# One stated order instead of a list scheduler: a three-stage kernel (LSH attention and two expert layers) on one core

## The chip, the cores and the metric

The kernel runs on one core of one Trainium2 chip. The time is that of the device in microseconds; the median of three runs before the change is 678.09 (677.57 to 679.59). Lower is better.

## The reference, cut to what matters

```
q_bits, k_bits = (q @ proj > 0), (k @ proj > 0)              # 6 hash bits each
mask   = bucket(q_bits)[:, None] == bucket(k_bits)[None, :]
scores = where(mask, q @ k.T / 8, -1e9)                      # 2 batches x 8 heads, 768 x 768, head 64
attn   = softmax(scores) @ v
x = attn as (1536, 512)
x = max(x @ w1, x @ w2, x @ w3) @ w_out                      # 512 -> 768 -> 512
h = x @ w_in                                                 # 512 -> 2048
return where(h > 0, h, exp(min(h, 0)) - 1) @ w_out2          # 2048 -> 512
```

The weights come as 64-bit floats, the attention inputs as 32-bit ones. The kernel splits every matmul operand in a high and a low half of 16 bits and sums three products.

## The kernel before, in words

The 1536 tokens are cut into six chunks (c = 0 to 5) of 256 tokens. A chunk's attention has 16 tiles (four pairs of heads, two heads, two blocks of 128 queries), so there are 96 tiles, t = 0 to 95. A tile goes through all engines: PE makes the scores (L681), DVE takes the row maximum (L684) and two small numbers of it (L685, L687), ACT the exponential (L689), ACT or DVE the high half (L693 to L697), POOL or DVE the low half (L700), the SP queue issues a DMA transpose of both halves (L702, `PT<-hl`), and PE multiplies by v (L711 to L713). After four tiles DVE divides, and the result is split again (L733, L734). After eight, a second transpose on SP (L737, `xT<-xn`) makes half of a chunk's input for the first expert layer.

The first expert layer of a chunk (L748, called with w13 and then wot; matmuls `mo<-xT,w` and `mo<-hT,wot`) can start when both xT halves of the chunk are there and the weights are unpacked: a load of 512 KB (L589), three to four operations on ACT and DVE that turn 64-bit words into 32-bit ones (L594 to L605), a sum of squares, and a split in two halves (L617 to L619). Its matmuls fill PE between the tiles of the following chunks. The second expert layer runs when attention is over: four groups of four blocks f, and for each group and chunk, four steps x (twelve matmuls, L748 `mo<-x1T,win`) and four steps o (six matmuls, L882). Between x and o of one block stand ACT (L867, L869), DVE (L870, L872), then the two halves (L874, L876). Its weights are loaded only when the tiles of attention have given their memory back.

All small results of PE go through a ring of three PSUM buffers, `mo`: a step that writes one waits until the third step before it has been read. In the second layer that reading ends with L872.

The program is built from a graph of 3,374 operations. Each has a dictionary of the engines that can do it (PE, V = DVE, A = ACT, G = POOL, D = the SP queue; for DMA loads and copies, D or the ACT queue), and a priority. `Graph.schedule` is a list scheduler: with costs written in the code (`vtt`, `act`, `gtt`, `pe`, a DMA model) it decides at every step which operation goes next and on which engine, and `emit` writes them in that order. Each engine then works strictly in this order and waits, by semaphores, for what its next instruction needs. DMA issues stand in the order of the queue that issues them: SP does nothing else, ACT issues between its own work. The loads of k, v and weights are held back until the first load of k has been issued (`g.after(..., first["kl"])`).

Of the kernel before, what the change touches and what calls it, by code (L numbers as in the profile page):

```python
# [21 lines left out]

# [8 lines left out]
class Graph:  # L37

    LAT = {"PE": 200, "V": 150, "A": 160, "G": 100, "D": 1500, "N": 0}
# [4 lines left out]
    def buf(self, pool, shape, dt, tag, bufs, ordered=False):  # L44

        self.bufs_of[tag] = bufs
        b = Buf(tag, lambda: pool().tile(shape, dt, tag=tag, name=tag, bufs=bufs))
        if ordered:
            b.turn = self.turns[tag]
            self.turns[tag] += 1  # L50
        return b
# [6 lines left out]
    def op(self, eng, fn, rd=(), wr=(), prio=0.0, two=False):  # L58

        i = len(self.ops)
        deps, allocs, used = set(), [], []
# [24 lines left out]
    def schedule(self):  # L88
        ops, n = self.ops, len(self.ops)
        engs = ("PE", "V", "A", "G", "D", "N")  # L90
        succ, left = [[] for _ in ops], [0] * n
        for o in ops:
            left[o["i"]] = len(o["deps"])
            for d in o["deps"]:
                succ[d].append(o["i"])
            for b in o["used"]:
                b.left = len(b.users)
        end, by, done = [0.0] * n, [None] * n, [False] * n
        rings, waiting = defaultdict(list), defaultdict(list)
        pending, ready, free = {e: [] for e in engs}, {e: [] for e in engs}, {e: 600.0 for e in engs}  # L100
        dma_free, dge, busy, warm = 0.0, 0.0, [], False
        held = {"V": 0.0, "G": 0.0}
        order = []

        def release(i, t0=0.0):
            for e in ops[i]["eng"]:
                r = max([t0] + [end[d] + self.LAT[by[d]] * (0.8 if by[d] == e else 1) for d in ops[i]["deps"]])
                heapq.heappush(pending[e], (r, i))

        for o in ops:  # L110
            if not left[o["i"]]:
                release(o["i"])
        while len(order) < n:
            best = None
            for e in engs:
                while pending[e] and (pending[e][0][0] <= free[e] or done[pending[e][0][1]]):
                    i = heapq.heappop(pending[e])[1]
                    if not done[i]:
                        c = ops[i]["eng"][e]
                        heapq.heappush(ready[e], (ops[i]["prio"] + (c[-1] if isinstance(c, tuple) and e != "D" else 0), i))  # L120
                while ready[e] and done[ready[e][0][1]]:
                    heapq.heappop(ready[e])
                t = free[e] if ready[e] else max(free[e], pending[e][0][0]) if pending[e] else None
                if t is not None and (best is None or t < best[0]):
                    best = (t, e)
            if best is None:
                stuck = {i for l in waiting.values() for i in l}
                msg = []
                for i in sorted(stuck):
                    for b in ops[i]["allocs"]:  # L130
                        r, k = rings[b.ring], self.bufs_of[b.ring]
                        if len(r) >= k and r[-k].left:
                            msg.append((i, ops[i]["prio"], b.ring, [(j, ops[j]["prio"], ops[j]["fn"].__qualname__[-30:], left[j]) for j in r[-k].users if not done[j]]))
                raise RuntimeError("no operation can start:" + "".join("\n  %s" % (m,) for m in msg[:60]))
            t, e = best
            if not ready[e]:
                free[e] = t
                continue
            if e == "V" and held["G"] > t:

                late_ = KAPPA * (held["G"] - t)
                j = min(range(len(ready[e])), key=lambda j: (ready[e][j][0] + late_ * ops[ready[e][j][1]]["two"], ready[e][j][1]) if not done[ready[e][j][1]] else (1e9, 0))
                _, i = ready[e][j]
                ready[e][j] = ready[e][-1]
                ready[e].pop()
                heapq.heapify(ready[e])
            else:
                _, i = heapq.heappop(ready[e])
            o = ops[i]
            if e == "V" and o["two"] and held["G"] > t or e == "G" and held["V"] > t:  # L150
                t1 = held["G" if e == "V" else "V"]
            else:
                t1 = t
            block = None
            for b in o["allocs"]:
                r, k = rings[b.ring], self.bufs_of[b.ring]
                if b.turn is not None and b.turn != len(r):
                    block = b.ring, b.turn
                    break
                if len(r) >= k:  # L160
                    old = r[-k]
                    if old.left:
                        block = old
                        break
                    if old.free > t:
                        block = old.free
                        break
            if block is not None:
                if isinstance(block, (Buf, tuple)):
                    waiting[block].append(i)  # L170
                else:
                    heapq.heappush(pending[e], (block, i))
                continue
            c = o["eng"][e]
            if e == "D" or (isinstance(c, tuple) and len(c) == 4):
                t0 = max(t, dge)
                free[e], dge = t0 + c[0], t0 + (c[1] if e == "D" else c[0])
                end[i] = max(dge + 650, dma_free) + c[2]
                dma_free = end[i]
                if not c[0]:  # L180
                    free[e] = max(t0 + 1300, end[i] - 877)
                lat = "D"
            else:
                c = c[0] if isinstance(c, tuple) else c
                if e == "PE":
                    busy = [(a, z) for a, z in busy if z > t - 3400]
                    share = sum(z - max(a, t - 3400) for a, z in busy) / 3400
                    warm = share > (0.5 if warm else 0.88)
                    c = c if warm else 2 * c
                    busy.append((t, t + c))  # L190
                free[e] = end[i] = t1 + c
                lat = e
                if e == "G" or e == "V" and o["two"]:
                    held[e] = t1 + c
            done[i], by[i] = True, lat
            order.append((i, e, t))
            for b in o["allocs"]:
                rings[b.ring].append(b)
                for j in waiting.pop((b.ring, len(rings[b.ring])), ()):
                    release(j, t)  # L200
            for b in o["used"]:
                b.left -= 1
                b.free = max(b.free, end[i] + self.LAT[lat])
                if not b.left:
                    for j in waiting.pop(b, ()):
                        release(j, b.free)
            for j in succ[i]:
                left[j] -= 1
                if not left[j]:
                    release(j)  # L210
        self.order, self.end = order, end
        return order

    def emit(self):
        for i, e, _ in self.schedule():
            o = self.ops[i]
            for b in o["allocs"]:
                b.ap = b.make()
            o["fn"](e)


# [17 lines left out]
def lsh_attention_moe_kernel(ctx: ExitStack, tc: tile.TileContext, q, k, v, proj,  # L239
# [53 lines left out]
    def ring(pool, shape, tag, bufs, dt=F32, ordered=False):  # L293
        p = pool if callable(pool) else (lambda: pool)
        return g.buf(p, list(shape), dt, tag, bufs, ordered)
# [133 lines left out]
    def plan_qk(kind, b, p, hf, u, prio):  # L429
# [26 lines left out]
        if u:  # L456
            g.after(lod, first["kl"])
# [84 lines left out]
    def plan_v(b, p, prio):  # L542
# [11 lines left out]
        g.after(lod, first["kl"])  # L554
# [26 lines left out]

    def plan_w(tag, src, prio, pool, nraw, n2, need=()):
# [6 lines left out]
        if tag == "w":  # L591
            g.after(ld, first["kl"])
            wloads.append(ld)
# [240 lines left out]
    def plan_moe2(c, gi, fs, p0, dp):  # L834
# [23 lines left out]
        outs = [ring(lambda: late["ps_out"], [128, 512], "out", 2 * QT) for _ in range(QT)]  # L858
        for m, f in enumerate(fs):
# [19 lines left out]
            def omm(e, f=f, m=m, gt=gt):  # L879
                for j in range(QT):  # L880
                    for pi, (x, y) in enumerate(((0, 0), (0, 1), (1, 0))):
                        PE.matmul(outs[j].ap, gt.ap[:, x, j * 128:(j + 1) * 128], wo2t[f].ap[:, y],  # L882
                                  start=(m == 0 and pi == 0), stop=(m == n - 1 and pi == 2))
# [119 lines left out]
```

## Time and profile before

| | |
|---|---|
| median of three runs | 678.09 us |
| span of the profiled execution, first to last instruction | 677.9 us |
| PE busy | 625.1 us (92%) |
| DVE busy | 578.8 us (85%) |
| ACT busy | 445.6 us (66%) |
| POOL busy | 204.3 us (30%) |
| DMA, mean over the span | 129 GB/s |
| first matmul of the first expert layer | 120.7 us |
| last tile's product with v | 360.7 us |

One execution is profiled. Its time beyond the span is not listed, the span and the median of the runs differ by 0.2 us. A busy PE is not PE at its peak, since the ends of matmuls are modelled and a lower clock lengthens them.

### The profile page before, as it was taken

What the parts mean: (1) busy time and instruction counts of PE and PEld (TensorE: products, weight loads), DVE (VectorE), ACT (ScalarE), POOL (GpSimd) and SP (SyncE); (2) the same over time, 40 slices, a digit from 0 to 9 for tenths busy, and PEclk for the clock granted to TensorE, in tenths of its full rate; (3) what the DMA queues carried; (4) which work ended last, traced back from release to release, by engine and by line L of the source; (5) the groups of instructions that cost most, each with busy time, mean ns of one, the idle gap of its engine ahead of it and who ended that gap; (6) DMA issues with size and microseconds to landing.
All of it is one profiled execution on the core that took longest, in us unless ns stands there. A gap on an engine that the chain in (4) does not pass through costs nothing.

```text
span 677.9 us, 16515 instructions
## 1 busy us (share of the span) xinstructions
PE 625.1 (92%) x6414; PEld 481.5 (71%) x6414; DVE 578.8 (85%) x1574; ACT 445.6 (66%) x807; POOL 204.3 (30%) x164
## 2 busy tenths in 40 slices
PE   5766567999999999999999799999999999999997
PEld 4645445787888888888889688766666666666664
DVE  7998799999979979989984997898899798877775
ACT  4788788898977846865562885676779365433331
POOL 0045444575666744665540011021020000000000
PEclk9958656999999999999999999999999999999999
DMA  9889998998798776989686544122121000000112
GB/s 281 254 214 207 215 250 204 234 213 157 149 193 177 134 140 111 157 165 163 139 179 175 179 153 156 33 94 63 49 78 62 1 1 1 1 1 1 63 51 74
DMA packets 201118, 87.65 MB, mean 129 GB/s; under 512 B 167760, under 2 KB 195408, under 8 KB 201040
## 3 DMA queue, kind: packets, MB, share of 16 engines
q1 hardware_dynamic: 187120, 68.78, 47.5%
q10 hardware_dynamic: 13920, 17.82, 8.9%
q8 instruction: 50, 0.82, 0.5%
q14 instruction: 28, 0.23, 0.1%
HBM read 38.80 MB, written 3.15 MB: 62 GB/s over the span
## 4 chain that ended last, share of the span: by engine, by line
PE 75%; DVE 9%; ACT 5%; DMA 4%; issue 2%; SPq 0%; ACTq 0%; POOL 0%; DVEq 0%; POOLq 0%
PE mo L748 42%; PE out L882 18%; PE s L681 7%; DMA PT<-hl 4%; DVE m L684 2%; ACT P L689 2%; PE o L711 2%; PE o L712 2%; PE o L713 2%; DVE w L619 1%; PE mo L474 1%; DVE dc2w L605 1%; ACT mo L594 1%; DVE dc L605 0%; SPq L702 0%
## 5 line engine op out<-in xcount | busy, mean ns | idle before, releaser
L700 POOL TENSOR_TENSOR hl<-P,hl 128x768 f16<-128x768 f32 x77 | 131.9, 1719 | 127.3 <-DVE hl L697 55.4
L748 PE MATMUL mo<-xT,w 128*128 128x256 f16 x1296 | 153.4, 274 | 0.1
L748 PE MATMUL mo<-x1T,win 128*128 128x256 f16 x1152 | 140.6, 272 | 0.0
L882 PE MATMUL out<-wo2t,gt 128*128 128x512 f16 x576 | 139.1, 379 | 0.0
L748 PEld LDWEIGHTS <-w 128*128 128x128 f16 x1296 | 123.7, 98 | 15.1 <-issue 0.2
L748 PEld LDWEIGHTS <-win 128*128 128x128 f16 x1152 | 111.0, 98 | 27.5
L689 ACT ACTIVATE P<-s,bias,scale 128x768 f32<-128x768 f32 x96 | 91.9, 986 | 38.8 <-DVE bias L687 29.6
L867 ACT ACTIVATE r<-mo,nih 128x256 f32<-128x256 f32 x96 | 45.1, 470 | 86.4 <-PE mo L748 84.5
L684 DVE TENSOR_REDUCE m<-s 128x1 f32<-128x768 f32 x96 | 89.6, 949 | 5.2 <-PE s L681 4.7
L882 PEld LDWEIGHTS <-gt 128*128 128x128 f16 x576 | 56.0, 98 | 48.5
L876 POOL TENSOR_TENSOR gt<-g,gt 128x256 f16<-128x256 f32 x28 | 20.3, 724 | 224.7 <-ACT gt L874 74.6
L711 PE MATMUL o<-vt,PT 128*128 128x65 f16 x576 | 66.2, 198 | 8.7 <-DMA PT<-hl 5.1
L695 ACT CAST hl<-P 128x768 f16<-128x768 f32 x72 | 59.3, 827 | 13.8 <-DMA PT<-hl 9.3
L681 PE MATMUL s<-ka,qa 128*128 128x384 f16 x192 | 53.1, 362 | 14.8 <-ACT P L689 14.5
L712 PE MATMUL o<-vt,PT 128*128 128x64 f16 x576 | 66.1, 199 | 0.0
L713 PE MATMUL o<-vt,PT 128*128 128x65 f16 x576 | 65.9, 198 | 0.0
L711 PEld LDWEIGHTS <-PT 128*128 128x128 f16 x576 | 55.8, 100 | 13.6 <-DMA PT<-hl 6.1
L712 PEld LDWEIGHTS <-PT 128*128 128x128 f16 x576 | 55.7, 101 | 3.3 <-issue 0.9
L713 PEld LDWEIGHTS <-PT 128*128 128x128 f16 x576 | 55.7, 102 | 0.0
L870 DVE TENSOR_SCALAR uu<-e,sg 128x256 f32<-128x256 f32 x96 | 35.3, 368 | 23.5 <-ACT e L869 23.0
L681 PE MATMUL s<-kb,qb 76*128 76x384 f16 x192 | 54.0, 366 | 0.0
L748 PE MATMUL mo<-hT,wot 128*128 128x256 f16 x432 | 50.2, 272 | 0.5 <-DVE zq L500 0.5
(195 smaller groups left out, 1109.2 us busy)
## 6 DMA issues: line engine op xcount, KB each, us to landing
raww<-in_moe_w_dram SPq DMA_DIRECT2D x12, 512.0 KB
raw<-in_moe_w_out_dram ACTq DMA_DIRECT2D x8, 512.0 KB
raw<-in_moe_w_in_dram SPq DMA_DIRECT2D x8, 512.0 KB
raw<-in_moe_w_in_dram ACTq DMA_DIRECT2D x8, 512.0 KB
raw<-in_moe_w_out_dram SPq DMA_DIRECT2D x8, 512.0 KB
raww<-in_moe_w_dram ACTq DMA_DIRECT2D x6, 512.0 KB
out_dram<-ot SPq DMA_DIRECT2D x12, 256.0 KB
rawk<-in_k_dram SPq DMA_DIRECT2D x6, 384.0 KB
```

Source lines behind the costliest of these rows:

```text
L681: PE.matmul(ps.ap[:, h, :NK], lh[0:n, h0 + i, j], rh[0:n, i, h * CH:(h + 1) * CH], start=first, stop=not first)
L684: op({"V": vred(S)}, lambda e: V.tensor_reduce(out=m.ap, in_=ps.ap[:, :, :NK], op=ALU.max, axis=AX.XY), rd=[ps], wr=[m], prio=t + 80.5)
L689: op({"A": act(S, ap=2) - 42}, lambda e: A.activation(out=P.ap.rearrange("p (c n) -> p c n", c=2), in_=ps.ap[:, :, :NK], func=AF.Exp, scal ...
L695: A.copy(hl.ap[:, 0], P.ap)
L700: op({"G": gtt(S), "V": (vtt(S), -109.46)}, lambda e: eng[e].tensor_tensor(out=hl.ap[:, 1], in0=P.ap, in1=hl.ap[:, 0], op=ALU.subtract), r ...
L711: PE.matmul(oo, pt.ap[:, kt], vt.ap[:, i, kt, :D + 1], start=(kt == 0), stop=False)
L712: PE.matmul(oo[:, :D], pt.ap[:, kt], vt.ap[:, i, kt, D + 2:], start=False, stop=False)
L713: PE.matmul(oo, pt.ap[:, NS + kt], vt.ap[:, i, kt, :D + 1], start=False, stop=(kt == NS - 1))
L748: PE.matmul(o, lh(kk, x), rh(kk, y), start=(kk == 0 and pi == 0), stop=(kk == n - 1 and pi == 2))
L867: op({"A": act(NQ, ap=1) - 42}, lambda e, m=m, o=o, r=r: A.activation(out=r.ap, in_=o.ap[:, :NQ], func=AF.Relu, scale=nih.ap[:, m:m + 1]), ...
L870: op({"V": vts(NQ)}, lambda e, m=m, ex=ex, uu=uu: V.tensor_scalar(out=uu.ap, in0=ex.ap, scalar1=-1.0, scalar2=sg.ap[:, m:m + 1], op0=ALU.a ...
L882: PE.matmul(outs[j].ap, gt.ap[:, x, j * 128:(j + 1) * 128], wo2t[f].ap[:, y], start=(m == 0 and pi == 0), stop=(m == n - 1 and pi == 2))
```

## The change

`Graph.schedule`, its costs of latency and the three `g.after(..., first["kl"])` are deleted. A table `ORDER` states for all 3,374 operations which comes next and on which engine, and `emit` follows it. The graph, the operations and the buffer rings are the same. The six matmuls of a step o set their first and last flag by the order in which steps come, since the blocks of a group may now come in any order.

```
-        for i, e, _ in self.schedule():
-            o = self.ops[i]
+        raw = zlib.decompress(base64.b85decode(ORDER))
+        n = len(raw) // 2
+        assert n == len(self.ops)
+        done = [False] * n
+        for lo, hi in zip(raw[:n], raw[n:]):
+            w = hi << 8 | lo
+            o, e = self.ops[w >> 3], ENGINES[w & 7]
+            assert e in o["eng"] and not done[o["i"]] and all(done[d] for d in o["deps"])
+            done[o["i"]] = True
             for b in o["allocs"]:
                 b.ap = b.make()
             o["fn"](e)
...
-        if u:
-            g.after(lod, first["kl"])
...
-            def omm(e, f=f, m=m, gt=gt):
+            def omm(e, f=f, gt=gt, outs=outs, seen=seen):
+                seen.append(f)
                 for j in range(QT):
                     for pi, (x, y) in enumerate(((0, 0), (0, 1), (1, 0))):
                         PE.matmul(outs[j].ap, gt.ap[:, x, j * 128:(j + 1) * 128], wo2t[f].ap[:, y],
-                                  start=(m == 0 and pi == 0), stop=(m == n - 1 and pi == 2))
+                                  start=(len(seen) == 1 and pi == 0), stop=(len(seen) == n and pi == 2))
```

What the table says, read out of its entries and set against the order that the list scheduler makes (before, after):

| | before | after |
|---|---|---|
| operations on another engine than before | | 377 |
| DMA loads and copies on the ACT queue, whole program | 56 | 14 |
| the same, ahead of the first matmul of the first layer | 24 | 5 |
| of these: weights, q and k, v, big copies, copies of hash bits, proj | 8, 4, 2, 2, 6, 2 | 1, 1, 0, 1, 0, 2 |
| weight loads ahead of the second xT on the DMA queues | 20 | 21 |
| loads of k, q, v and transposes PT ahead of it | 7, 7, 6, 19 | 7, 7, 6, 19 |
| loads ahead of the first PT | 23 | 20 |
| tiles with scores on PE ahead of the first layer's first matmul | 26 | 26 |
| ahead of it on DVE: L464, L603, L734, L561 | 7, 14, 2, 4 | 2, 7, 0, 1 |
| ahead of it on DVE: L700, L618 | 2, 1 | 4, 6 |
| ahead of it on POOL: L464, L700, L734 | 3, 20, 2 | 8, 18, 4 |
| weights unpacked (L605), split (L619) ahead of it | 20, 17 | 18, 15 |
| sums of squares of second-layer weights on PE ahead of the last chunk's first matmul | 6 | 4 |
| steps x with just two steps of PE between them and the x that held their `mo` buffer | 2 | 12 |
| steps o with just three steps of PE after their x | 1 | 10 |

Ten or so smaller operations ahead of the first layer change between DVE and ACT in either direction.

## Rows read from the trace of the kernel before

**Rows 1.** Windows: stretch, length, busy of engines (instructions), clock, DMA share, GB/s.

```profile
0.00:120.70 120.70, 79.85 (x919) 58.69 (x919) 105.26 (x291) 93.88 (x151) 41.81 (x39) 0.76 0.97 232
...
120.70:361.00 240.30, 236.64 (x3198) 202.48 (x3194) 215.92 (x520) 174.41 (x267) 137.12 (x93) 1.00 0.85 163
361.00:390.00 29.00, 24.63 (x240) 21.62 (x237) 21.38 (x55) 17.30 (x38) 1.20 (x1) 0.99 0.66 195
390.00:674.60 284.60, 284.02 (x2073) 198.76 (x2071) 235.97 (x710) 159.97 (x353) 24.20 (x31) 0.99 0.16 51
```

**Rows 2.** Line L748: PE instructions, shortest/median/longest ns, first and last start.

```profile
L748 PE MATMUL mo<-xT,w x1296: 269/272/421, 120.7 to 415.7; 128*128 128x256 f16 x186
```

**Rows 3.** Chain that ended last, 0 to 120.7: shares by line, longest DMA piece.

```profile
by line: DVE m L684 9.4%; PE s L681 7.0%; DMA PT<-hl 6.9%; issue 6.6%; DVE w L619 6.1%; ACT P L689 4.9%; DVE dc2w L605 4.6%; ACT mo L594 3.6%; SPq L702 2.5%; PE mo L474 2.0%; ACTq L528 1.7%; DVE scale L685 1.6%; ACT hl L695 1.5%; DVE dc2w L
...
76.29 8.31 DMA PT<-hl
```

**Rows 4.** Groups of instructions by form: count, busy us, mean ns, idle before.

```profile
L464 DVE TENSOR_TENSOR natk<-rawk,natk 128x768 f16<-128x768 f32 x5 | 5.6, 1121 | 0.0
L603 DVE TENSOR_SCALAR dc2w<-raww 128x512 uint16<-128x512 uint16 x15 | 6.5, 450 | 0.0
L734 DVE TENSOR_TENSOR xn<-xf,xn 128x256 f16<-128x256 f32 x9 | 7.7, 855 | 0.1
L561 DVE TENSOR_SCALAR vt<-rawv,vs 128x768 f16<-128x768 f32 x6 | 4.3, 716 | 0.0
L700 DVE TENSOR_TENSOR hl<-P,hl 128x768 f16<-128x768 f32 x19 | 21.4, 1124 | 0.9 <-ACT hl L695 0.5
L618 DVE TENSOR_SCALAR wo2t<-dc,o2s 128x512 f16<-128x512 f32 x5 | 2.4, 483 | 0.1
L605 DVE SCALAR_TENSOR_TENSOR dc2w<-mo,dc2w 128x512 int32<-128x512 int32 x24 | 16.3, 686 | 1.3 <-ACT dc2w L598 1.1
L619 DVE SCALAR_TENSOR_TENSOR w<-dc2w,swm,w 128x512 f16<-128x512 f32 x18 | 16.5, 937 | 1.6 <-ACT w L617 1.5
L464 POOL TENSOR_TENSOR natq<-rawq,natq 128x512 f16<-128x512 f32 x6 | 7.4, 1228 | 8.2 <-DVE natq L462 6.3 <-ACT P L689 1.9
L876 DVE TENSOR_TENSOR gt<-g,gt 128x256 f16<-128x256 f32 x68 | 29.2, 429 | 1.7
```

**Rows 5.** DMA issues on the ACT queue: sequencer's time, shortest/median/longest ns.

```profile
L589 ACTq DMA_DIRECT2D raww<-in_moe_w_dram x6: 374/374/449, 5.8 to 92.5; - x6
...
L528 ACTq DMA_DIRECT2D kb<-btk x8: 730/771/1513, 38.7 to 249.5; - x8
```

**Rows 6.** Windows with almost only loads, and with three transposes and nothing else.

```profile
13.00:30.00 17.00, 11.80 (x164) 9.62 (x164) 16.18 (x46) 11.93 (x24) 0.00 (x0) 1.00 1.00 284
...
214.40:219.90 5.50, 5.50 (x62) 4.58 (x61) 5.12 (x13) 3.43 (x7) 2.06 (x2) 1.00 0.89 202
```

**Rows 7.** Timeline of PE at the seam: start, length, instruction [idle before, releaser].

```profile
387.23 0.18 PE L342 MATMUL mo<-w2acc,ones 128*128 128x1 bf16 x1 [0.99 <-DVE hx L802]
...
389.08 0.18 PE L342 MATMUL mo<-w2acc,ones 128*128 128x1 bf16 x1 [1.65 <-DVE o2s L380]
```

**Rows 8.** Timeline of the second layer: a quick block and a slow one.

```profile
472.50 1.47 PE L748 MATMUL mo<-x1T,win 128*128 128x256 f16 x12
...
475.11 1.47 PE L748 MATMUL mo<-x1T,win 128*128 128x256 f16 x12
...
475.36 0.48 DVE L872 SCALAR_TENSOR_TENSOR g<-mo,aj,uu 128x256 f32<-128x256 f32 x1
...
441.08 1.47 PE L748 MATMUL mo<-x1T,win 128*128 128x256 f16 x12
...
445.44 0.47 DVE L872 SCALAR_TENSOR_TENSOR g<-mo,aj,uu 128x256 f32<-128x256 f32 x1
...
446.28 0.43 DVE L876 TENSOR_TENSOR gt<-g,gt 128x256 f16<-128x256 f32 x1
```

**Rows 9.** Waits, 390 to 674: total us, times, longest.

```profile
ACT r L867 <- PE mo L748: 84.5, 61, 1.8
```

More of the change, by code (lines that the diff above doesn't have):

```diff
@@ L1 @@
-import heapq
+import base64
+import zlib
 from collections import defaultdict
@@ L37 @@
 class Graph:
-    LAT = {"PE": 200, "V": 150, "A": 160, "G": 100, "D": 1500, "N": 0}
     def __init__(self):
@@ L47, in buf @@
         b = Buf(tag, lambda: pool().tile(shape, dt, tag=tag, name=tag, bufs=bufs))
-        if ordered:
-            b.turn = self.turns[tag]
-            self.turns[tag] += 1
         return b
@@ L86, in after @@
         self.ops[i]["deps"].update(js)
[L88 to L212, printed above, removed]
@@ L553, in plan_v @@
            wr=[raw, acc], prio=prio + 176.2)
-        g.after(lod, first["kl"])
         qloads.append((lod, (b * NH * NP + p) + 0.0 / UL))
@@ L591, in plan_w @@
         if tag == "w":
-            g.after(ld, first["kl"])
             wloads.append(ld)
@@ L858, in plan_moe2 @@
         outs = [ring(lambda: late["ps_out"], [128, 512], "out", 2 * QT) for _ in range(QT)]
+        seen = []
         for m, f in enumerate(fs):
```

50 lines of the change are left out of this document (added).

## The prediction, made before the changed kernel was run

> **What bounds the kernel now.** I read the windows by stage first, because the shares of the whole span mix three stages. From 120.7 us to 361 PE is busy 236.64 of 240.30 at full clock, and from 390 to 674.6 it is busy 284.02 of 284.60 [rows 1]. In these two stages only PE's own work counts, and the change does not touch it: the same matmuls, the same shapes. What PE loses lies in two other places. The first is the head, up to the first matmul of the first expert layer at 120.7 [rows 2]: PE is busy 79.85 us there at a mean clock of 0.76. The second is the seam from 361 to 390, with 24.63 of 29.00 busy. So a new order can win time only in these two, and it can lose time anywhere.
>
> What bounds the head? DVE is busy 105.26 of 120.70, ACT 93.88, and the DMA engines 0.97 of it at 232 GB/s [rows 1]. Nothing has much room. The chain that ended last says which of them is felt: the four DVE lines that its header still shows make 21.7% of the stretch (9.4, 6.1, 4.6, 1.6), ACT's waits at its own DMA issues (L528) 1.7%, and one transpose alone takes 8.31 us, from 76.29 on [rows 3]. So DVE first, then ACT with its queue, and transfers at one place.
>
> I make the sum against the span of 677.9; the median of the runs is 678.09, so 0.2 us lie around it, and I add nothing for them.
>
> **The head: DVE.** Counted in the table ahead of the first layer's first matmul, DVE gives away five low halves of q and k (L464, 1.121 each), seven sign operations (L603, 0.450), two low halves of results (L734, 0.855) and three scalings of v (L561, 0.716): 5.6 + 3.2 + 1.7 + 2.1 = 12.6 us. It takes on two low halves of tiles (L700, 1.124) and five weight splits (L618, 0.483): 2.2 + 2.4 = 4.7. Two weights less are unpacked (L605, 0.686) and two less split (L619, 0.937) by then: 3.2 us that move behind 120.7, where PE sets the pace and DVE has 24 us free of 240 [rows 1, 4]. Net 12.6 - 4.7 + 3.2 = 11.1 us less. The smaller moves go both ways and I leave them out. How much of it is felt? At least the share of the chain, 0.22, which gives 2.4; at most DVE's busy share, 105.26 of 120.70 or 0.87, which gives 9.7. I take half, 5.5, since the header is cut and DVE's other lines on the chain are missing in the lower figure.
>
> **The head: ACT's queue.** Nineteen issues leave it. Thirteen at 0.374 and the six copies of hash bits at 0.771 are 4.9 + 4.6 = 9.5 us of ACT's sequencer [rows 5]. They go to SP, where the transposes stand in the same order. ACT's computing stays about the same (eight operations taken on, seven splits given away). At most 9.5 are felt; at least what the chain names, 1.7% of 120.7 or 2.1 us, since all six bit copies go. I take 2.1: ACT is a fifth below the span [rows 1].
>
> **The head: transfers.** The bytes ahead of the second xT are the same but for one weight load. Is there room for an earlier xT? Loads run at 284 GB/s when almost alone, and three transposes with nothing beside them take 5.50 x 0.89 / 3 = 1.63 us each [rows 6]. From the shapes of the tiles: 20 weights of 0.524 MB, 7 of k and 6 of v of 0.393, 7 of q of 0.262, together 17.4 MB or 61 us; 19 transposes, 31 us; two xT of two thirds, 2 us. That makes 94 us, plus the small copies, of the 120 that they have. The bound of one more load is 0.524 / 284, 1.8 us, and I cost it at nothing because the 26 us of slack cover it. If the cover is gone, the load costs all of its 1.8.
>
> [...]
>
> **The head: POOL.** It does five more low halves of q and k, two more of results and two fewer of tiles: five operations more. An operation of one form takes 0.855 on DVE in the attention stage (L734) and 0.429 in the second layer (L876), where POOL is busy 24.20 of 284.60 [rows 1, 4]. So a DVE operation beside POOL is stretched by 0.43, and five of them cost 2.1 us. The lower end is nothing, if DVE happens to do other things; I take 2.1, since L734 is of this stage.
>
> [...]
>
> Head: 5.5 + 2.1 - 2.1 = 5.5 us won.
>
> **The seam.** PE waits 0.99 and 1.65 us for sums of squares of second-layer weights, at 387.23 and 389.08, before the last chunk's first matmul [rows 7]. In the table four such sums stand ahead of it instead of six; the two others come behind it, while matmuls of the last chunk run. I take both waits off, 2.6 us. At the other end the four can be as late as the six were, and nothing is won.
>
> **The second layer.** Here the new order is tighter than the old. At twelve places a step x has two PE steps (2.61 us, as the starts 472.50 and 475.11 of two steps x show, with one o between) between the end of the step that held its `mo` buffer and its own start, and at ten places a step o starts three steps, half as much again or 3.9 us, after its x; before there were two and one. The x of 472.50 ends at 473.81, half of 2.61 later, and has its buffer read (L872) at 475.84, 2.0 us later; its low half (L876) follows some 0.8 after that, if it goes as in the slow block. The slow one of 441.08 ends at 442.39 in the same way and needs 3.5 us for the one (445.91) and 4.3 for the other (446.71) [rows 8]. A quick block fits in both distances; a slow one makes PE wait 0.9 or 0.4. Between 0 and 12 x 0.9 + 10 x 0.4 = 14.8 us. In 61 of 96 blocks ACT was waiting for PE when x ended [rows 9], so most are quick, and I take a tenth, 1.5.
>
> Sum: 677.9 - 5.5 - 2.6 + 1.5 = **671.3**. For the runs I say 671, with its own range from 667 to 676 (the head between 2 and 10 us won, the seam between 0 and 2.6).
>
> **Rivals.**
> - *Transfers set the head.* Against: the 94 us above. For: a DMA share of 0.97 and the transpose of 8.31 us [rows 1, 3]; on SP twenty of 21 loads now stand ahead of transposes in one queue. Then the first layer starts no earlier, only seam and second layer count, and one more load may: 677.9 - 2.6 + 1.5 = 676.8, up to 678.6.
> - *The second layer stalls* (slower). The mechanism is the ring of `mo`: if most blocks there are slow, PE waits 14.8 us, and 677.9 - 8.1 + 14.8 = 684.6. It decides when the 22 places wait 0.37 us on average (8.1 / 22). For it: unpacking of weights shares ACT and DVE with these blocks. Against: DVE has 48 us free of 285 [rows 1].
> [...]
> - *Everything in the head that waits gets shorter.* If DVE's 11.1 is felt in full, and the transpose of 8.31 falls to about half as no other queue loads beside it, the head wins 11.1 + 2.1 - 2.1 + 4.2 = 15.3 and the end is 661.5.
>
> **How the numbers follow.** My forecast 0.55, transfers 0.11, a stalling second layer 0.11, POOL 0.08, the shorter head 0.15. The bound of a difference that a measurement of this kernel can tell is 0.3%, 2 us, so faster is below 676.1. Faster: 0.55 + 0.15 + 0.07 of POOL, 0.77. Same: nearly all of the transfers, 0.10. Slower: the stalling layer and what is left of the others, 0.13. The range runs from 662, which leaves out half of the shorter head, to 680, which leaves out most of the stalling layer: two in ten at most.
>
> **What would show it.** Right: the first matmul of L748 starts at about 115 instead of 120.7; DVE is busy some 10 us less before it, the ACT queue issues five loads or copies there; no wait of PE over half a microsecond for L380 or L395 before the last chunk's first matmul; from then to the end PE is idle no more than 2 us. Wrong: L748 starts at 120 or later with SP waiting at a load in front of transposes; PE waits for L872 or L876 in the second layer; DVE's operations on 128x768 grow longer. The prediction would be wrong most of all if PE, from its first L748 on, is no longer fed without gaps, since the middle stage has almost no idle PE today and any hole there adds to the end.

## The result: slower, and where the time went

The changed kernel takes 686.84 us (median, 686.51 to 688.95), beside 677.84 of the kernel before on the same chip: a ratio of 1.0128, with an interval from 1.0103 to 1.0153. The forecast was 671, faster, with a range up to 680. Sign and range were both wrong.

In the kernel after, L663 is what L748 was, L684 the evacuation of the first layer's `mo` (L769 before), L617 the transpose (L702), L534, L533, L514 and L518 the weights' lines L619, L618, L599 and L603. I read the windows again, now with the middle stage cut at 145, 160 and 180 us. First the kernel after (stretch, length, busy of PE, PEld, DVE, ACT and POOL with instructions, clock, DMA share, GB/s):

```profile
0.00:120.70 120.70, 79.43 (x905) 59.19 (x905) 105.30 (x272) 92.49 (x143) 47.84 (x45) 0.70 0.95 228
120.70:145.00 24.30, 21.71 (x275) 17.73 (x272) 23.09 (x60) 21.28 (x34) 11.70 (x7) 1.00 0.90 198
145.00:160.00 15.00, 11.52 (x134) 9.11 (x133) 8.88 (x20) 9.45 (x16) 9.86 (x7) 0.77 0.84 164
160.00:180.00 20.00, 19.07 (x304) 16.61 (x302) 19.33 (x44) 15.96 (x26) 9.42 (x6) 1.00 0.61 115
180.00:361.00 181.00, 177.47 (x2331) 150.62 (x2329) 153.80 (x384) 128.70 (x198) 103.50 (x71) 1.00 0.82 156
361.00:390.00 29.00, 27.70 (x341) 24.80 (x338) 15.29 (x35) 14.18 (x28) 7.59 (x7) 1.00 0.69 178
390.00:670.00 280.00, 277.48 (x2074) 197.32 (x2072) 229.76 (x693) 168.33 (x382) 37.95 (x52) 1.00 0.18 56
```

The same three short stretches of the kernel before:

```profile
120.70:145.00 24.30, 23.57 (x304) 20.02 (x300) 23.52 (x55) 20.91 (x33) 15.11 (x11) 1.00 1.03 227
145.00:160.00 15.00, 15.00 (x233) 13.05 (x232) 13.58 (x38) 13.33 (x21) 9.53 (x8) 1.00 0.94 179
160.00:180.00 20.00, 19.03 (x262) 16.49 (x260) 19.71 (x53) 18.46 (x30) 12.92 (x9) 1.00 0.72 142
```

The head is no shorter: PE is busy 79.43 us by 120.7, as against 79.85 [rows 1]. The loss begins behind it. From 120.7 to 160 PE is busy 33.23 us instead of 38.57, so 5.3 us of idle time are new, and from 145 to 160 its mean clock is 0.77 instead of 1.00. In windows of 5 us (PE's busy time, clock, DMA share and GB/s):

```profile
145.00:150.00 5.00, 3.25 (x60) 1.00 1.10 255
150.00:155.00 5.00, 3.27 (x15) 0.51 0.86 111
155.00:160.00 5.00, 5.00 (x61) 0.81 0.56 127
```

The clock stood at 1.00 and falls within an idle stretch (it is 0.54 from 150 to 151 us, where PE does nothing, 0.50 from 151 to 156 and 1.00 again from 157 on); twelve matmuls of L663 take 1.47 us from 144.84 on and 2.74 from 151.73. By estimate from the windows, 3.27 us at 0.51 and 5.00 at 0.81 cost 3.27 x 0.49 + 5.00 x 0.19 = 2.6 us of PE's work. Idle time and clock make 7.9 of the 9.3 us between the two spans (687.2 and 677.9). The rest is idle time too: 1.6 us more from 180 to 361 us and 0.7 more in the head and the second layer, 0.7 less at the seam. What PE waited for, from 120 to 165 us (total, times, longest):

```profile
PE mo L663 <- DVE hx L684: 3.5, 1, 3.5
PE s L596 <- ACT P L604: 1.9, 2, 1.2
PE o L626 <- DMA PT<-hl: 0.6, 1, 0.6
```

One wait of 3.5 us, from 148.25 to 151.73, stands out. The timeline of DVE shows how it comes about:

```profile
144.96 0.68 DVE L520 SCALAR_TENSOR_TENSOR dc2w<-mo,dc2w 128x512 int32<-128x512 int32 x1
147.07 0.31 DVE L420 TENSOR_REDUCE zq<-mo 128x48 f32<-128x144 f32 x1 [1.43 <-PE mo L415]
147.30 0.42 DVE L382 TENSOR_SCALAR natq<-rawq 128x512 f16<-128x512 f32 x1
147.63 1.83 DVE L425 TENSOR_SCALAR bitsq<-zq 128x96 f16<-128x96 f32 x1
149.20 0.97 DVE L518 TENSOR_SCALAR dc2w<-raww 128x512 uint16<-128x512 uint16 x1
...
150.14 0.94 DVE L599 TENSOR_REDUCE m<-s 128x1 f32<-128x768 f32 x1
151.00 0.67 DVE L684 SCALAR_TENSOR_TENSOR hx<-mo,hx 128x512 f32<-128x512 f32 x1
```

The matmuls that fill this `mo` buffer end at 146.3. Its evacuation (L684) could run then: DVE is idle from 145.6 to 147.07. But the table puts six other instructions ahead of it, and the first of them (L420) waits for a matmul of PE (L415). PE in turn had waited 0.6 us, up to 144.28, for a transpose that stands ahead of that matmul in its list. The chain of waits has this transpose as its longest piece here:

```profile
135.44 2.30 issue
137.74 6.49 DMA PT<-hl
```

And SP's timeline says why it was issued only then:

```profile
131.05 5.09 SPq L505 DMA_DIRECT2D raww<-in_moe_w_out_dram  x2
136.26 4.37 SPq L617 DMA_TRANSPOSE PT<-hl  x2
```

with SP's waits from 128 to 147 us:

```profile
SPq L617 <- POOL hl L615: 6.8, 5, 2.5
SPq L505 <- DVE dc2w L518: 4.1, 1, 4.1
```

Two loads of weights keep SP from 131.05 to 136.14. The second stands there 4.1 us until DVE has read its buffer (L518), and two transposes stand behind it, whose inputs were ready at 133.2 and 135.4. The larger figure, 6.8 us for POOL's low halves, is no difference: the kernel before has it too, 6.8 us in the same stretch, but no load that waits for a buffer. So lists that are each served strictly in order hand a delay on: DVE to SP, SP to PE, PE to DVE, DVE back to PE. The old schedule had the same operations in another order and no wait over 0.7 us there.

### The profile page after: what moved, and what is told of

It reads as the page before. It is cut to its first block, busy times and chain, and to the rows that moved or that the text cites. A ratio compares the mean times of both kernels' runs of the same rounds, so it can differ in the third digit from the quotient of the medians.

```text
span 687.2 us, 16546 instructions
## 1 busy us (share of the span) xinstructions
PE 627.7 (91%) x6414; PEld 482.4 (70%) x6414; DVE 563.2 (82%) x1519; ACT 453.1 (66%) x829; POOL 229.4 (33%) x197
## 4 chain that ended last, share of the span: by engine, by line
PE 62%; DVE 23%; DMA 7%; issue 3%; ACT 2%; SPq 1%; POOL 1%; DVEq 0%; ACTq 0%; POOLq 0%
PE mo L663 34%; PE out L799 18%; DVE m L599 5%; PE s L596 4%; DMA PT<-hl 3%; DVE w L534 2%; PE o L626 1%; PE o L627 1%; PE o L628 1%; DVE dc2w L520 1%; DVE hx L684 1%; DVE scale L600 1%; DVE hl L615 1%; DMA qb<-qa 1%; DMA rawq<-in_q_dram 1%
## 5 line engine op out<-in xcount | busy, mean ns | idle before, releaser
L615 POOL TENSOR_TENSOR hl<-P,hl 128x768 f16<-128x768 f32 x79 | 135.3, 1717 | 125.9 <-ACT hl L610 72.1
L663 PE MATMUL mo<-xT,w 128*128 128x256 f16 x1296 | 154.6, 274 | 4.4 <-DVE hx L684 3.7
L663 PEld LDWEIGHTS <-w 128*128 128x128 f16 x1296 | 124.4, 98 | 22.6 <-DVE hx L684 3.6
L663 PE MATMUL mo<-x1T,win 128*128 128x256 f16 x1152 | 136.6, 273 | 0.0
L799 PE MATMUL out<-wo2t,gt 128*128 128x512 f16 x576 | 134.8, 379 | 0.0
L663 PEld LDWEIGHTS <-win 128*128 128x128 f16 x1152 | 111.7, 98 | 24.5
L604 ACT ACTIVATE P<-s,bias,scale 128x768 f32<-128x768 f32 x96 | 94.6, 988 | 51.6 <-DVE bias L602 34.6
L792 POOL TENSOR_TENSOR gt<-g,gt 128x256 f16<-128x256 f32 x51 | 35.7, 700 | 226.3 <-ACT gt L790 115.5
L599 DVE TENSOR_REDUCE m<-s 128x1 f32<-128x768 f32 x96 | 90.9, 949 | 14.1 <-PE s L596 13.6
L626 PE MATMUL o<-vt,PT 128*128 128x65 f16 x576 | 67.8, 202 | 6.3 <-DMA PT<-hl 4.7
L627 PE MATMUL o<-vt,PT 128*128 128x64 f16 x576 | 67.6, 203 | 0.0
L628 PE MATMUL o<-vt,PT 128*128 128x65 f16 x576 | 67.4, 201 | 0.0
L626 PEld LDWEIGHTS <-PT 128*128 128x128 f16 x576 | 57.2, 103 | 10.4 <-DMA PT<-hl 6.2
L610 ACT CAST hl<-P 128x768 f16<-128x768 f32 x69 | 56.9, 827 | 8.6 <-DMA PT<-hl 7.5
L627 PEld LDWEIGHTS <-PT 128*128 128x128 f16 x576 | 57.2, 103 | 2.6 <-issue 1.0
L628 PEld LDWEIGHTS <-PT 128*128 128x128 f16 x576 | 57.2, 104 | 0.0
L663 PE MATMUL mo<-hT,wot 128*128 128x256 f16 x432 | 50.1, 273 | 0.7 <-DVE p2c L302 0.7
```

The lines of the kernel that those rows point to most:

```text
L599: op({"V": vred(S)}, lambda e: V.tensor_reduce(out=m.ap, in_=ps.ap[:, :, :NK], op=ALU.max, axis=AX.XY), rd=[ps], wr=[m], prio=t + 80.5)
L604: op({"A": act(S, ap=2) - 42}, lambda e: A.activation(out=P.ap.rearrange("p (c n) -> p c n", c=2), in_=ps.ap[:, :, :NK], func=AF.Exp, scal ...
L610: A.copy(hl.ap[:, 0], P.ap)
L615: op({"G": gtt(S), "V": (vtt(S), -109.46)}, lambda e: eng[e].tensor_tensor(out=hl.ap[:, 1], in0=P.ap, in1=hl.ap[:, 0], op=ALU.subtract), r ...
L626: PE.matmul(oo, pt.ap[:, kt], vt.ap[:, i, kt, :D + 1], start=(kt == 0), stop=False)
L627: PE.matmul(oo[:, :D], pt.ap[:, kt], vt.ap[:, i, kt, D + 2:], start=False, stop=False)
```

## The experiments

Four theories are named in the expectations. Order: the wait for the evacuation, with the clock behind it, is the loss. Queue: loads on SP delay transposes. POOL: its operations stretch DVE's. Debt: the table reaches the first layer with attention work undone. The times of the kernel before beside the runs were 678.1 to 678.8, so ratios are compared.

**Where the loss lies: one order spliced into the other.** `table` and `schedule` are the lists of (operation, engine).

```diff
 a_head:  table up to the first L663 step, then what is left of schedule
 b_head:  schedule up to that step, then what is left of table
 b_to_n0: schedule up to the first step of hT x wot (169.8 us), then table
```

> The table up to and with the first matmul step of the first expert layer, then the old schedule's order, engines and queues for all that is left. Order theory (the loss is made by the list behind that step): 678 to 680, the 1 us by which the step is late and no more. Debt theory (the table reaches that step with attention work left undone, V step 8 being 8 us late, and the middle pays for it): 683 to 688.

> The reverse: the old schedule up to and with the first matmul step of the first expert layer, then the table. Order theory: 685 to 687, with the wait near 148 us still there. Debt theory: 675 to 679, because the middle then starts from the old state and only the seam and the second layer are the table's.

> The old schedule up to and with the first matmul step of the first layer's output product (169.8 us), then the table. It prices the table behind the stretch in question. By the prediction's terms (seam 2.6 us won, second layer 1.5 us lost): 676 to 677. If the table is neutral there: 678. If its loss were spread over the whole middle: 681 to 685.

Measured: a_head 686.55 (ratio 1.0114, 1.0077 to 1.0151), b_head 685.64 (1.0091, 1.0052 to 1.0130), b_to_n0 679.40 (1.0013, 0.9996 to 1.0029). With the old head in front the table still loses, and PE's wait for L684 is still there (3.41 us at 143.6). With the old schedule up to 169.8 us the loss is gone. So it is made between 120.7 and 170 us, and seam and second layer together win nothing that can be measured. The time of a_head lies in the range of the debt theory, but it doesn't test the table's own middle: the splice opens a wait of its own (3.35 us at 123.7, PE's clock 0.79 over 120.7 to 145), behind an unpacking step on DVE (L517 there), as the table had left weights to unpack which the old order expects to be done.

**Parts of the change put back alone.** `old` is the engine that the schedule had chosen; "D" is SP's queue, "G" POOL.

```diff
+a_queue: [(i, old[i] if "D" in (e, old[i]) else e) for i, e in table]
+a_pool:  [(i, old[i] if "G" in (e, old[i]) else e) for i, e in table]
```

> The table's order, but the DMA issues that it moved from ACT's queue to SP (and the few that it moved the other way) are back on the queue they had before; nothing else differs. Queue theory (loads on SP delay the transposes behind them, and the late transposes open the gaps of PE): near 678 to 680, the pieces of transposes on the chain gone. POOL theory and order theory: the gaps come from DVE, so 685 to 688, or worse by the 0.37 to 0.77 us that each issue costs ACT.

> The table's order, but every operation that changed between POOL and another engine is back on the engine it had before (149 on POOL instead of 182). POOL theory (the sum of squares L425 took 1.83 us and the tile operation L518 0.97 beside POOL, so the evacuation that PE waits for came late): the wait of 3.48 us at 148 us and the low clock behind it go, 679 to 682. Queue theory: 686 to 688. Order theory: 685 to 688, since the evacuation stays behind the same operations.

Measured: a_queue 713.71 (1.0517, 1.0452 to 1.0582), a_pool 709.96 (1.0439, 1.0378 to 1.0500). No theory had figures like these. It looks as if order, engines and queues of a list fit only each other: an engine put back leaves the instruction at a place in the other engine's list that was made without it. The traces were not followed to where these two lose the rest. Still, a_pool tells one thing: up to 180 us it goes like the table (PE busy 52.10 of 59.30 at 0.94 from 120.7 to 180, the table 52.30 at 0.94), with POOL's extra work gone, and PE waits 3.5 us for the same evacuation. So that extra work is not what makes the hole.

**The hole itself: one DVE instruction moved, four DMA issues moved, both.**

```diff
 a_evac, DVE's list:
  L520 dc2w<-mo,dc2w
+ L684 hx<-mo,hx
  L420 zq<-mo
  ...
  L599 m<-s
- L684 hx<-mo,hx
 a_pt, SP's list:
- L505 raww (waits for its buffer)
  L617 PT<-hl
  L617 PT<-hl
+ L505 raww
- L401 qb<-qa, L448 qb<-btq
  L617 PT<-hl
+ L401 qb<-qa, L448 qb<-btq
  ... and one L617, ready at 112.0, ahead of L372 rawq and L505 raww
```

> The table with one DVE instruction moved: the evacuation of the tenth matmul step of the first expert layer (hx<-mo, L684, at 151.00 us) stands six DVE instructions earlier, right behind the L520 that ran at 144.96; every other engine's list is untouched. [...] Queue theory and POOL theory, or lateness of the whole list: the hole opens at another place, 684 to 687.

> The table with four DMA issues moved behind transposes on SP's queue: the weight load that blocks SP from 131.6 to 135.8 us for its buffer now stands behind two transposes that were ready at 133.2 and 135.4, one transpose that was ready at 112.0 moves ahead of a load of q and a weight, and two small copies move behind another transpose. Queue theory (late transposes open the gaps of PE): 679 to 683. Order theory: the evacuation that PE waits for stays where it is, so the hole stays and the time is 685 to 688.

> Both edits, the moved evacuation and the four moved DMA issues. Order theory: no better than the moved evacuation alone by more than the few gaps of 0.6 to 1.2 us that wait for transposes, 676 to 680. Queue theory: the sum of both, 672 to 677.

Measured: a_evac 683.22 (1.0072, 1.0047 to 1.0096), a_pt 681.48 (1.0044, 1.0022 to 1.0066), both 683.49 (1.0065, 1.0039 to 1.0090). Against the table's 1.0128 the one instruction won 0.56%, 3.8 us, and the four issues 0.84%, 5.7 us; by the two intervals each difference is good to about 0.35%. Only a_pt lies in the range of a theory (queue); a_evac lies below the 684 to 687 of a hole that opens elsewhere, and the two edits together above both of their ranges. In a_evac PE no longer waits for L684, and its clock stays at 1.00:

```profile
145.00:160.00 15.00, 14.21 (x220) 11.84 (x217) 14.75 (x33) 11.77 (x19) 11.50 (x9) 1.00 0.77 151
```

L425 still takes 1.83 us there, beside POOL's L615, and nobody waits for it. In a_pt the transposes go first, and the same wait for L684 shrinks to 1.3 us with the clock at 1.00:

```profile
130.91 4.03 SPq L617 DMA_TRANSPOSE PT<-hl  x2
134.99 0.57 SPq L505 DMA_DIRECT2D raww<-in_moe_w_out_dram  x1
135.68 2.53 SPq L617 DMA_TRANSPOSE PT<-hl  x1
```

So order and queue theory are two ends of one chain: the wait goes when the evacuation is moved, and shrinks when the transposes come earlier. a_pt moves four issues at once, and which of them won is not separated. The two edits don't add up: with both, PE waits 2.1 us for `xT` at 120.8 and 1.4 us for a DVE operation at 157.9. Neither gets back all of the 1.28%. From 120.7 to 180 us PE is idle 1.7 us in the kernel before, 7.0 under the table, 5.6 in a_evac, 3.1 in a_pt and 5.5 with both, and only under the table does the clock fall there. So a_evac wins the clock's 2.6 us and 1.4 of idle time, 4.0 beside the 3.8 measured, since other waits opened as the large one went; a_pt wins 2.6 + 3.9 = 6.5 beside 5.7. What each still lacks lies mostly in the same stretch, in waits of 0.3 to 2.1 us that differ between the three.

**The price of a hole, in the old schedule.** An evacuation on ACT (the fourth of the first layer) is repeated; all else is the kernel before.

```diff
-A.activation(out=t.ap, in_=o.ap, func=AF.Copy, scale=CX)
+for _ in range(7 if c == 0 and f == 2 else 1): A.activation(out=t.ap, in_=o.ap, func=AF.Copy, scale=CX)
```

> The kernel before with one evacuation on ACT (hx<-mo at 137.8 us, first layer) done seven times over instead of once: 3.6 us more on ACT, and PE waits that much longer for the buffer. Nothing else differs. If a hole of PE costs its length: 680.5 to 682. [...] If PE's backlog covers it: 678.

> The same with the evacuation done three times: a hole of 1.2 us. If a hole costs its length and no more: 679. If this one too takes the clock down: 682 to 684. By the gaps of 1.1 to 1.3 us in the runs with the clock at 1.00 around them, 679 is what I expect.

Measured: seven times 681.97 (1.0062, 1.0038 to 1.0086), three times 680.07 (1.0020, 1.0001 to 1.0039). The profiled execution with seven, at 684.61 the longest, shows PE's wait, and its clock in windows of 5 us:

```profile
142.78 0.80 PE L681 MATMUL s<-ka,qa 128*128 128x384 f16 x2 [3.00 <-ACT P L689]
```

```profile
140.00:145.00 5.00, 2.21 (x22) 0.72 0.70 190
145.00:150.00 5.00, 5.00 (x51) 0.60 1.04 220
150.00:155.00 5.00, 5.00 (x83) 1.00 0.91 143
```

That is the table's picture in the old order: a wait of 3 us, then 5 us at a clock of 0.60. By the same estimate two of the 5 us windows lose 2.21 x 0.28 + 5.00 x 0.40 = 2.6 us to the clock, as many as in the table. The median, 681.97, lies at the upper end of the range for a hole that costs its length only (680.5 to 682); its 4.2 us (2.6 to 5.8) lie between the hole alone, 3.0, and hole plus clock, 5.6. So the price of the clock is shown for the profiled executions and not for the median; whether the clock falls in each execution I can't tell from one profile. Three times is covered: PE has no wait behind it in the profile, and the 1.4 us (0.1 to 2.6) are hardly apart from none. I had expected a hole of 1.2 us there, and there was none to price.

**Is it DVE's load?** The third step of the weights' unpacking does 8 of 512 columns.

```diff
-out=t2.ap, in0=t1.ap.bitcast(I32), scalar=3, in1=t2.ap,
+out=t2.ap[:, :8], in0=t1.ap.bitcast(I32)[:, :8], scalar=3, in1=t2.ap[:, :8],
```

> The kernel before with the third step of every weight's unpacking (L605, 0.69 us on DVE, 24 weights and 19 of them before the first expert layer) done on 8 of 512 columns only, so that the weights are wrong; same order, same waits. DVE has about 11 to 12 us less to do in the head. If DVE's work is felt there with a share of one half, as the prediction took it: 672 to 673. If a share of 0.87: 668. If the head is set by something else: 676 to 678.

> The table with the third step of every weight's unpacking (L520) done on 8 of 512 columns, so that the weights are wrong; the same order and waits. DVE loses 11 us ahead of the first expert layer and about 3 us between its first step and 170 us. In the old order the same edit won 4 us. If the table's loss is too much work on DVE: it wins the 9 us of the loss as well, 673 to 677. If the loss is a chain of waits (transpose, PE's list, DVE's list), DVE's relief helps here about as it did before, by 3 to 6 us: 681 to 684.

Measured: b_or8 674.29 (0.9930, 0.9891 to 0.9969), a_or8 679.76 (1.0015, 0.9994 to 1.0037). In the old order 19 such steps shrink from 0.685 to 0.158 us, 10.0 us of DVE ahead of the first layer, and 0.70% or 4.7 us (2.1 to 7.4) come out of it: a share of 0.47 (0.2 to 0.7). Under the table the edit wins 1.1%, more than I allowed the chain theory and less than I allowed DVE's load. But the hole is untouched, with DVE idle in front of it:

```profile
140.90 0.31 DVE L420 TENSOR_REDUCE zq<-mo 128x48 f32<-128x144 f32 x1 [1.97 <-PE mo L415]
141.46 1.82 DVE L425 TENSOR_SCALAR bitsq<-zq 128x96 f16<-128x96 f32 x1
...
144.82 0.67 DVE L684 SCALAR_TENSOR_TENSOR hx<-mo,hx 128x512 f32<-128x512 f32 x1
```

```profile
145.56 0.82 PE L663 MATMUL mo<-xT,w 128*128 128x256 f16 x3 [3.47 <-DVE hx L684]
```

The wait is 3.47 us as before, with some 10 us less work on DVE. So it is made by the order of the lists, not by DVE's load.

**The queues alone, in the old order.**

```diff
+b_qsp:      [(i, new[i] if "D" in (e, new[i]) else e) for i, e in schedule]
+b_qsp_head: the same for the 26 issues from ACT to SP up to 169.8 us
+b_qsp_rest: the same for the 28 issues behind it
```

> The kernel before, in its own order and with its own engines, but each DMA issue stands on the queue that the table gives it (49 from ACT to SP, 7 from SP to ACT). It prices the queues alone. By the prediction's term (ACT freed of its issues): 676. Queue theory (an order made for two queues has its loads ahead of the transposes when they share one): slower, 681 to 690, with transposes late behind loads in the trace. If order and queues can't be exchanged one by one, as putting the queues back under the table suggested (713.7): 690 or more.

> The kernel before with only the 26 DMA issues of the head and of the first chunk moved from ACT to SP (up to 170 us). If the gain of the queues lies in the head (the trace of all 56 moves has the first expert layer 2 to 4 us earlier and some of it lost again between 360 and 390 us): 674 to 676.5. If the 56 moves won by other things: 678.

> The kernel before with only the 28 DMA issues behind 170 us on the queues that the table gives them. If the gain lies in the head: 678 to 680, the seam's waits longer by up to 2 us. If it lies here: 676.5.

Measured: b_qsp 676.89 (0.9974, 0.9951 to 0.9996), b_qsp_head 676.29 (0.9953, 0.9930 to 0.9977), b_qsp_rest 678.68 (0.9999, 0.9973 to 1.0025). The old order with 26 issues moved from ACT to SP beats both kernels, by 3.2 us the one before (1.6 to 4.8). So one queue for loads and transposes is no harm by itself. What stands out in the table is a load that waits for its buffer in front of transposes that are ready (a_pt).

## Why the prediction was wrong

**The step that failed** is in the part on what bounds the kernel: in the middle stage "only PE's own work counts, and the change does not touch it". The whole stage was costed at nothing, and it lost 5.3 us of idle time from 120.7 to 160 and 2.6 us of clock. In the old order no wait of PE there is over 0.7 us; the change rewrote all the lists, and one of them put an evacuation six places too late. That the order behind the first step makes the loss is shown by b_head and b_to_n0; that this chain carries a large part of it by a_evac and a_pt (3.8 and 5.7 of the 9 us), and that DVE's load does not make it by a_or8. The last sentence on what would make the prediction wrong most of all named this, but no rival and no chance stood for it; the slower rival was put into the second layer. Of the 16 us between the forecast, 671.3, and the span of 687.2, this stage makes 9.5 (with the 1.6 idle from 180 to 361), the head 5.9 and the seam 1.9; the second layer gave back 1.2. So the sign was lost here, but the 5.5 us forecast for the head did not come either.

**The head, DVE.** Forecast 5.5 us won: 11.1 us less work, of which half is felt. The half agrees with b_or8 (0.47, but 0.2 to 0.7). The 11.1 did not show: DVE's busy time by 120.7 is 105.30 us, 105.26 before [rows 1], with 19 instructions fewer. The groups of the head by form (count, busy us, mean ns, idle before) show what filled the gap, first before, then after:

```profile
L619 DVE SCALAR_TENSOR_TENSOR w<-dc2w,swm,w 128x512 f16<-128x512 f32 x17 | 14.3, 863 | 1.6 <-ACT w L617 1.5
...
L599 DVE TENSOR_SCALAR dc2w<-raww 128x512 uint16<-128x512 uint16 x11 | 4.7, 448 | 0.0
L562 DVE SCALAR_TENSOR_TENSOR vt<-rawv,vs,vt 128x768 f16<-128x768 f32 x4 | 4.0, 1009 | 0.0
```

```profile
L534 DVE SCALAR_TENSOR_TENSOR w<-dc2w,swm,w 128x512 f16<-128x512 f32 x14 | 14.4, 1039 | 0.2 <-ACT w L532 0.2
...
L514 DVE TENSOR_SCALAR dc2w<-raww 128x512 uint16<-128x512 uint16 x10 | 7.4, 752 | 0.4 <-DMA raww<-in_moe_w_dram 0.4
L481 DVE SCALAR_TENSOR_TENSOR vt<-rawv,vs,vt 128x768 f16<-128x768 f32 x4 | 5.3, 1324 | 0.0
```

These three alone grew by 14 x 0.176 + 10 x 0.304 + 4 x 0.315 = 6.8 us. The prediction took 2.1 us of stretch beside POOL. The two traces tell what stretched them, when each instruction is sorted by whether one of POOL ran beside it (mean us, count):

| | before, alone | before, beside POOL | after, alone | after, beside POOL |
|---|---|---|---|---|
| L619, now L534 | 0.743 (11) | 1.084 (6) | 0.742 (8) | 1.437 (6) |
| L599, now L514 | 0.448 (11) | none | 0.450 (3) | 0.881 (7) |
| L562, now L481 | 1.004 (3) | 1.024 (1) | 1.013 (2) | 1.635 (2) |

Alone they take the same in both kernels; only those beside POOL grow. Take for every DVE instruction up to 120.7 us what it lasts beyond the median of its line and form without POOL: by this estimate the stretch is 7.1 us before and 14.2 after, and the rest of the durations falls from 122.1 to 110.7, by 11.4. So the count of 11.1 held, and the term that was mis-sized is POOL's: 7.1 us instead of 2.1. The last 4.3 are in no term: the durations add up to 4.3 less than before, but DVE's instructions also overlap by 4.3 less, so its busy time stays. POOL's five extra operations are not needed for it: a_pool has none of them, and the same lines take 0.741 alone and 1.364 beside POOL (L531), 0.486 and 1.085 (L511) in its head. Which of DVE's instructions stand beside POOL's is made by the order.

At one place the stretch can be read off. L425 takes 1.83 us, ten of its form 0.380 at the median, and POOL's L615 runs from 147.33 for 1.88, so that both end within 0.3 us. Its stretch, 1.83 less 0.38 or some 1.4 us, held up nobody in a_evac and the evacuation in the table: what a stretched operation costs hangs on who stands behind it.

**The head, ACT's queue.** Forecast 2.1 us. In the old order the 26 issues moved up to 170 us won 3.2 (1.6 to 4.8), which bears the term out in size. That they won it in the head is not shown: the profiled execution of b_qsp_head, its slowest, has its first step at 120.6 us, like the kernel before. Under the table the term can't be told apart. Only one of the six loads of [rows 5] (L589, now L505) is left on ACT's queue. What counted here was a load that blocks its own queue, SP's, for 4.1 us.

**The head as a whole.** The first matmul of L663 starts at 121.8 us, forecast 115:

```profile
L663 PE MATMUL mo<-xT,w x1296: 268/273/418, 121.8 to 430.1; 128*128 128x256 f16 x186
```

Six profiles have the old order in the head (before, b_head, b_to_n0, b_hole6, b_hole2, b_qsp_rest): they reach it at 117.7 to 120.7, at 119.1 on the mean. Three have the table's (this one, a_head at 120.3, a_evac at 119.9), at 120.7 on the mean. So being 1 us later is no finding, but nothing is left of 5 us won.

**The seam.** Forecast 2.6 us won. PE's waits there, before (361 to 390) and after (370 to 402):

```profile
PE mo L342 <- ACT junk L395: 1.7, 3, 0.7
PE mo L342 <- DVE o2s L380: 1.7, 1, 1.7
PE mo L342 <- DVE hx L802: 1.0, 1, 1.0
```

```profile
PE mo L264 <- ACT junk L317: 2.2, 3, 1.1
PE mo L663 <- DVE o2s L302: 0.7, 1, 0.7
PE mo L264 <- DVE hx L684: 0.7, 1, 0.7
```

4.4 us became 3.6: the waits for L802 and L380 that [rows 7] show, 2.6 us, have 1.4 us in their place, and the waits for L395 grew. The term was mis-sized: 0.8 instead of 2.6. That fewer sums ahead of the last chunk shortened the waits is likely but was not tested alone; b_to_n0 shows no gain in the end of the kernel.

**The second layer.** Forecast 1.5 us lost, and a rival with 14.8. From 402 us to the end PE waits 0.2 us in all. The shorter distances in `mo` that I counted cost nothing.

**The other rivals.** That transfers set the head was not tested by itself; the 4.7 us that b_or8 won by less work on DVE speak against it. But its clause on loads ahead of transposes in one queue named the first link of the chain that was found; its price was looked for in the head, and it fell due in the middle stage. The chance of 0.08 for POOL stood for its five operations costing DVE more than 2.1 us; that they cost it POOL's whole time is shown by no run. The traces show, by the estimate above, 7.1 us more stretch than before, and not from those five: a_pool has none of them, and the same line takes 1.364 beside POOL there and 0.741 alone.

**Two slips in the sum.** The time of a run lies some 1.8 us above the span, not 0.2: 688.95 and 687.2 us here, and so in every run that lists both. So the span of 677.9 must belong to the slowest of the three runs before, 679.59. The profiled execution of the kernel after is the slowest of its four as well, so the two spans can be compared. And the own range of 667 to 676 leaves out the second layer's 1.5 us at its upper end, which comes to 677.4. Neither changes the outcome.

What stays open: of the 9 us, a_evac and a_pt each recover part, and no run recovered all with the table's order. Nor is it tested by a run of its own that POOL's work stretched DVE's in the head; it is read from the traces.

## What to carry to other kernels

A stage in which the bound engine has no gaps is not safe from a new order (from 145 to 160 us PE was busy 15.00 of 15.00 us before and 11.52 after): its fullness is made by evacuations and transfers that come in time, so follow, for each buffer that it reuses, where the instruction that frees it stands in its engine's list, and what those ahead of it wait for. A transfer that waits for a buffer, here 4.1 us, must not stand in an in-order queue ahead of one that is ready and awaited; a_pt, which moves it and three other issues, won 5.7 us. Do not price an instruction by its mean in the old order either: what stands beside it changes with the order, as L599, now L514, took 0.448 us on average in the head before and 0.752 after. And when a list is frozen, engines and order may not come apart: putting one part back cost 21 us (POOL) and 26 us (queues) on top of the table's 9, by the ratios.

## What was not expected of the hardware

In or right behind waits of PE of 3.0 to 3.5 us the granted clock fell from 1.00: in the table to 0.51 and 0.81 in two stretches of 5 us, in a_or8 to 0.50 from 145 to 150 us, in b_hole6 to 0.72 and 0.60, in b_head to 0.56 and 0.76, and it came back while PE was busy without a gap (in the table to 1.00 at 157 us, with PE busy 10.00 of 10.00 us from 155 to 165). After waits of 1.3 us (a_pt) and 2.1 us (both edits) it stayed at 1.00; behind the two waits of [rows 7], 0.99 and 1.65 us, it was 0.51 from 389.6 to 393 us in the kernel before. So these traces show no one length of a wait from which it falls. In the table and in b_hole6 the hole cost, by the estimates above, some 2.6 us more than its length in the execution that was profiled.
